# The first weight load of a decode layer, split into 16 and 112 partitions

## The chip, the cores and the metric

The kernel runs on one core of a Trainium2 chip. The metric is the device time of one execution in microseconds; shown is the median of several runs. A profile is one more execution with the hardware profiler on. Its span runs from the first to the last instruction of the program, and the time of that execution is slightly longer than the span.

## The reference

One decode step of a transformer layer with attention and a gated MLP side by side, all in float32, for one token `x` of 1024 elements:

```python
xn = _layernorm(x, axis=-1)
# A: attention over the last W = 4096 of 65536 cached positions, 32 query heads, 4 key/value heads
q = (xn @ wq)                                  # wq: 1024 x 4096
k, v = k_cache[:, :, Sk - W:, :], v_cache[:, :, Sk - W:, :]
p = softmax(q k^T * Dh ** -0.5)
a = (p v) @ wo                                 # wo: 4096 x 1024
# B: GEGLU
h = gelu(xn @ w_gate) * (xn @ w_up)            # both 1024 x 3584
b = h @ w_down                                 # 3584 x 1024
return x + a + b
```

With one token every weight is used once, so some 94 MB are read from HBM for each execution.

## The kernel before

All weights and the window of the two caches pass through one SBUF tensor, `ring`, of 128 partitions and 176 KB in each. The list `pieces` names the loads in order, with kind, index, place in the ring and size per partition in KB: `q` 0 and `q` 1 (the two halves of `wq`, 8 MiB each), `k` 0, `g` 0 (`w_gate`), `v` 0, `k` 1, `g` 1, `u` 0 (`w_up`), `v` 1, `u` 1, `o` 0 and 1 (`wo`), and the pieces `d` of `w_down`. `load` issues the DMA of a piece on SP's queue (through `dma`, L219), and `pump` issues as many pieces as find their place in the ring free; `done` frees a piece's place and pumps again. So SP's queue has a fixed order, and an instruction in it waits until the engines have done with what stood in that place. At the start `q` 0, `q` 1 and `k` 0 fit at once; `g` 0 takes the place of `q` 0.

The half `q` 0 is 512 rows of `wq`. `rows` puts four of them in each partition, so a partition receives one run of 4 x 4096 floats, 64 KB:

```python
    def rows(w, a):
        return w[512 * a:512 * (a + 1), :].rearrange("(p r) n -> p (r n)", r=4)
```

`project("q", 0)` multiplies it with the normed token on VectorE (DVE): for each of the four rows in a partition one instruction over 128 x 4096 adds the row times a scalar per partition to the accumulator `part` (the first a TENSOR_SCALAR at L209, the others a SCALAR_TENSOR_TENSOR at L213). `project("q", 1)` does the same with the second half, `projected("q")` adds up over the partitions on TensorE, and the queries go on to the scores.

`Program` records every operation with the regions that it reads and writes, and works out from the regions which earlier operations it has to wait for. Each DMA has a semaphore of its own (`s_dma` and its number among the operations), and a reader of a region waits for every DMA that wrote a part of it.

Of the kernel before, what the change touches and what calls it, by code (L numbers as in the profile page):

```python
# [10 lines left out]
P = 128  # L11
# [135 lines left out]
def decode_layer(nc, x, k_cache, v_cache, wq, wo, w_gate, w_up, w_down, out):  # L147
# [69 lines left out]
    def dma(engine, o, i, reads=(), writes=(), tag=None):  # L217
        return prog.add(
            engine, lambda e: e.dma_start(o, i), list(reads), list(writes), dma=True, tag=tag  # L219
        )  # L220
# [4 lines left out]
    def rows(w, a):  # L225
        return w[512 * a:512 * (a + 1), :].rearrange("(p r) n -> p (r n)", r=4)

    def heads_of(a):
        return wo[2048 * a:2048 * (a + 1), :].rearrange("(p t) n -> p (t n)", p=P)
# [14 lines left out]
    def load(kind, i, at, size):  # L244
        slot = ring[:, at * KB:(at + size) * KB]
        held[kind, i] = slot
        if kind == "v":
            src = v_cache[0, 2 * i:2 * i + 2, SK - WIN:, :].rearrange("g (p j) d -> p g (j d)", p=P)
            dma("sp", slot.rearrange("p (g n) -> p g n", g=2), src, writes=[slot], tag=(kind, i))
        elif kind == "k":  # L250
            src = k_cache[0, 2 * i:2 * i + 2, SK - WIN:, :].rearrange("g (s j) d -> s g (j d)", g=2, j=64)
            dma("sp", slot, src, writes=[slot], tag=(kind, i))
        elif kind == "d":
            lo, hi = i
            halves = 2 if lo == TD - 1 else 1
            wide = slot.rearrange("p (t n) -> p t n", n=D)
            for half in range(halves):
                cols = slice(half * D // halves, (half + 1) * D // halves)
                dst = wide[:, :, cols]
                dma("sp", dst, hidden_rows[:, lo:hi, cols], writes=[dst], tag=(kind, i, half))  # L260
        else:
            src = {
                "q": lambda: rows(wq, i), "g": lambda: rows(w_gate, i), "u": lambda: rows(w_up, i),
                "o": lambda: heads_of(i),
            }[kind]()
            dma("sp", slot, src, writes=[slot], tag=(kind, i))

    queue = list(pieces)
    live = {}
# [1 line left out]
    def pump():  # L271
        while queue:
            kind, i, at, size = queue[0]
            if any(at < hi and lo < at + size for lo, hi in live.values()):
                return
            load(*queue.pop(0))
            live[kind, i] = (at, at + size)
# [436 lines left out]
    for half in range(2):  # L714
        half_on_pe(column(27), held["d", (27, 28)], half, False, True)
        add(y[:, half, :], acc[:, half, :P], x_out[:, half, :])
        for k, engine in enumerate(("sp", "act")):
            src = y[31 + 64 * k:33 + 64 * k, half, :]
            dma(
                engine, stores[0, half, 2 * k:2 * k + 2, :], src, reads=[src],  # L720
                tag=("out", half, k),
# [26 lines left out]
```

## Time and profile before

| | |
|---|---|
| median of 3 runs | 226.75 us (226.56 to 226.86) |
| the profiled execution | 226.83 us, its span 225.5 us |
| bytes read from HBM | 94.38 MB, 419 GB/s over the span |
| busy DVE, PE, ACT | 143.2, 87.5, 26.3 us |
| SP's DMA queue (q1) | 97.5% of 16 DMA engines over the span |
| the two `A_wq` issues on SP | 0.41 us each |

The page's slices are fortieths of the span, with busy shares in tenths. In the chain of waits each piece stands with its start, its length, and what it was: a transfer, an engine's work at a line, or "issue", in which nothing shown was waited for. In the timeline the bracket behind a row gives how long the engine was idle before it and what ended that.

### The profile page before, as it was taken

To read this page: it belongs to the slowest core of one execution; us is meant where nothing else is said; L and a number is where in the kernel's file an instruction comes from. 1 tells how busy PE (TensorE), PEld (TensorE's weight loads), DVE (VectorE), ACT (ScalarE), POOL (GpSimd) and SP (SyncE) were. 2 spreads that over 40 slices of the span, in tenths; PEclk is the share of its full clock that TensorE was granted. 3 is DMA by queue.
4 is the path that set the end of the run, shared out by engine and by line. 5 is a ranking of instruction groups with operands and counts; after the bars stand their busy time and mean duration, and the time that the engine had idled before them with its cause. 6 is when DMAs were issued, how large, how long until landed. Compare 5 with 4: busy or idle time off the path is not lost.

```text
span 225.5 us, 1396 instructions
## 1 busy us (share of the span) xinstructions
PE 87.5 (39%) x574; PEld 34.8 (15%) x574; DVE 143.2 (64%) x127; ACT 26.3 (12%) x45; POOL 0.7 (0%) x6
## 2 busy tenths in 40 slices
PE   1200000007699007989002537137339204408475
PEld 0100000006263002462000111011002001002131
DVE  7500998499727990000998699869538804938691
ACT  2000000004555001482000300200000000000000
POOL 1000000000000000000000000000000000000000
PEclk9999999999999755999755667857855855965889
DMA  9899899899989999999999998999999999999992
GB/s 373 372 395 535 372 395 535 349 405 478 468 349 426 465 401 503 427 397 471 427 397 392 433 509 387 478 391 491 419 395 488 419 395 413 427 439 442 382 405 111
DMA packets 3317, 94.46 MB, mean 419 GB/s; under 512 B 350, under 2 KB 366, under 8 KB 1008
## 3 DMA queue, kind: packets, MB, share of 16 engines
q1 hardware_dynamic: 3288, 94.38, 97.5%
q8 instruction: 4, 0.07, 0.1%
q10 hardware_dynamic: 24, 0.01, 0.0%
q14 instruction: 1, 0.01, 0.0%
HBM read 94.38 MB, written 0.00 MB: 419 GB/s over the span
## 4 chain that ended last, share of the span: by engine, by line
DMA 65%; DVE 26%; PE 7%; issue 1%; SPq 1%; DVEq 0%
DVE part L213 24%; DMA ring<-in_B_w_down 19%; DMA ring<-in_A_wq 18%; DMA ring<-in_B_w_gate 15%; DMA ring<-in_A_wo 13%; PE acc L158 3%; PE tp L163 2%; PE s_p L158 2%; DVE part L209 1%; SPq L219 1%; DVE rows_sb L186 0%; DVE part L189 0%; DVEq L118 0%; SPq L118 0%
## 5 line engine op out<-in xcount | busy, mean ns | idle before, releaser
L213 DVE SCALAR_TENSOR_TENSOR part<-ring,xz,part 128x3584 f32<-128x3584 f32 (+1 forms) x19 | 78.8, 4148 | 26.6 <-DMA ring<-in_B_w_gate 22.6
L163 PE MATMUL tp<-ident,ring 128*128 128x128 f32 x128 | 20.3, 303 | 44.4 <-DMA ring<-in_A_k_cache 42.8
L213 DVE SCALAR_TENSOR_TENSOR part<-ring,oz,part 128x1024 f32<-128x1024 f32 x15 | 19.3, 1285 | 9.9 <-DMA ring<-in_A_wo 9.4
L172 ACT ACTIVATE ring<-tp 128x512 f32<-128x512 f32 x32 | 18.1, 596 | 58.4 <-PE tp L163 58.0
L163 PEld LDWEIGHTS tp<-ident,ring 128*128 128x128 f32 x128 | 15.0, 152 | 51.2 <-DMA ring<-in_A_k_cache 42.9
L209 DVE TENSOR_SCALAR part<-ring,xz 128x3584 f32<-128x3584 f32 (+1 forms) x3 | 6.5, 2176 | 19.7 <-DMA ring<-in_A_wq 12.1
L158 PE MATMUL acc<-ring,oz 128*32 128x512 f32 x64 | 11.7, 899 | 16.8 <-DMA ring<-in_A_wo 16.8
L213 DVE SCALAR_TENSOR_TENSOR part<-ring,hz,part 128x1024 f32<-128x1024 f32 x10 | 12.8, 1285 | 6.1 <-DMA ring<-in_B_w_down 5.8
L158 PE MATMUL acc<-part,unit 128*32 128x448 f32 (+1 forms) x48 | 7.3, 742 | 22.3 <-DVE part L213 22.3
L158 PE MATMUL o_p<-ring,pT 128*32 128x512 f32 x64 | 11.0, 847 | 7.1 <-DMA ring<-in_A_v_cache 6.5
L158 PE MATMUL acc<-ring,hz 128*32 128x128 f32 (+1 forms) x60 | 8.0, 616 | 10.1 <-DMA ring<-in_B_w_down 10.1
L158 PE MATMUL s_p<-ring,qz 128*32 128x512 f32 x64 | 9.3, 598 | 0.0
L163 PE MATMUL tp<-ident,rows_sb 128*128 128x128 f32 x16 | 3.5, 361 | 12.0 <-ACT rows_sb L172 11.8
L158 PE MATMUL sums<-ring,hz 128*32 128x256 f32 x72 | 6.2, 482 | 4.7 <-DMA ring<-in_B_w_down 4.7
L158 PEld LDWEIGHTS acc<-ring,oz 128*32 128x32 f32 x64 | 2.5, 155 | 26.6 <-DMA ring<-in_A_wo 19.4
L158 PEld LDWEIGHTS acc<-part,unit 128*32 128x32 f32 x48 | 1.4, 126 | 26.4 <-DVE part L213 24.2
L172 ACT ACTIVATE rows_sb<-s_p,negm 128x512 f32<-128x512 f32 x2 | 1.4, 687 | 30.4 <-DVE negm L209 30.4
L158 PEld LDWEIGHTS o_p<-ring,pT 128*32 128x32 f32 x64 | 2.6, 149 | 14.5 <-issue 13.4
L158 PE MATMUL acc<-ring,xz 128*32 128x448 f32 x32 | 4.8, 767 | 0.0
L158 PEld LDWEIGHTS acc<-ring,hz 128*32 128x32 f32 x60 | 2.2, 135 | 15.8 <-issue 14.0
L163 PEld LDWEIGHTS tp<-ident,rows_sb 128*128 128x128 f32 x16 | 2.3, 179 | 15.5 <-ACT rows_sb L172 13.6
L158 PEld LDWEIGHTS sums<-ring,hz 128*32 128x32 f32 x72 | 2.4, 136 | 9.2 <-DMA ring<-in_B_w_down 7.3
(85 smaller groups left out, 47.8 us busy)
## 6 DMA issues: line engine op xcount, KB each, us to landing
ring<-in_B_w_gate SPq DMA_DIRECT2D x2, 7168.0 KB, 31.9
ring<-in_B_w_up SPq DMA_DIRECT2D x2, 7168.0 KB, 33.9
ring<-in_A_k_cache SPq DMA_DIRECT2D x2, 4096.0 KB, 39.7
ring<-in_A_v_cache SPq DMA_DIRECT2D x2, 4096.0 KB, 34.8
ring<-in_B_w_down SPq DMA_DIRECT2D x1, 6144.0 KB, 42.9
ring<-in_B_w_down SPq DMA_DIRECT2D x1, 4096.0 KB, 38.8
ring<-in_B_w_down SPq DMA_DIRECT2D x2, 1024.0 KB, 40.4
ring<-in_B_w_down SPq DMA_DIRECT2D x3, 512.0 KB, 42.0
```

The costliest lines, as they stand in the source:

```text
L158: "pe", lambda e: e.matmul(o, lhsT, rhs, start=start, stop=stop),
L163: prog.add("pe", lambda e: e.transpose(o, i, eye), [i, eye], [o])
L172: "act", lambda e: e.activation(o, i, func, scale=scale, **kw),
L209: dve(lambda e: e.tensor_scalar(o, i, s1, s2, op0=op0, **kw), reads, [o])
L213: lambda e: e.scalar_tensor_tensor(o, i, factor, other, op0=ALU.mult, op1=ALU.add),
L219: engine, lambda e: e.dma_start(o, i), list(reads), list(writes), dma=True, tag=tag
```

## The change

The load of `q` 0, the first of the kernel, is issued as two transfers: partitions 0 to 15 (1 MiB), then partitions 16 to 127 (7 MiB). All other loads go as before.

```diff
-            dma("sp", slot, src, writes=[slot], tag=(kind, i))
+            cuts = [0, 16, P] if (kind, i) == ("q", 0) else [0, P]
+            for lo, hi in zip(cuts, cuts[1:]):
+                dma("sp", slot[lo:hi, :], src[lo:hi, :], writes=[slot[lo:hi, :]], tag=(kind, i))
```

On SP, at the head of the program, the order with the shape of each transfer (partitions x elements) is, before:

```order
L219 DMA ring<-in_A_wq 128x16384 [waits barrier_Pool_Activation_PE_DVE_SP_release]
L219 DMA ring<-in_A_wq 128x16384
L219 DMA ring<-in_A_k_cache 128x1x8192
L219 DMA ring<-in_B_w_gate 128x14336 [waits s_dve]
L219 DMA ring<-in_A_v_cache 128x2x4096 [waits s_dve]
```

and now:

```order
L219 DMA ring<-in_A_wq 16x16384 [waits barrier_Pool_Activation_PE_DVE_SP_release]
L219 DMA ring<-in_A_wq 112x16384
L219 DMA ring<-in_A_wq 128x16384
L219 DMA ring<-in_A_k_cache 128x1x8192
L219 DMA ring<-in_B_w_gate 128x14336 [waits s_dve]
```

One transfer more stands ahead of `q` 1. On DVE, where the projection of `q` begins, the difference is:

```order
 L195 TENSOR_TENSOR st<-st 128x1 [waits s_dve]
 L209 TENSOR_SCALAR xz<-xc,st 128x8 [waits s_dve]
-L209 TENSOR_SCALAR part<-ring,xz 128x4096 [waits s_dma4,s_dve]
+L209 TENSOR_SCALAR part<-ring,xz 128x4096 [waits s_dma4,s_dma5,s_dve]
 L213 SCALAR_TENSOR_TENSOR part<-ring,xz,part 128x4096 [waits s_dve] x3
-L213 SCALAR_TENSOR_TENSOR part<-ring,xz,part 128x4096 [waits s_dma5,s_dve]
+L213 SCALAR_TENSOR_TENSOR part<-ring,xz,part 128x4096 [waits s_dma6,s_dve]
```

The first instruction that reads `q` 0 waits for both of its transfers (`s_dma4` and `s_dma5`); all later DMA semaphores have a number one higher, and nothing else moves.

## The prediction

> **What bounds the kernel now.** I read the page first, for what is busy from end to end.
>
> ```profile
> span 225.5 us, 1396 instructions
> DMA  9899899899989999999999998999999999999992
> q1 hardware_dynamic: 3288, 94.38, 97.5%
> DMA 65%; DVE 26%; PE 7%; issue 1%; SPq 1%; DVEq 0%
> ```
>
> The transfers fill every slice to 0.8 or more until the last one, nearly all of them on queue q1, the one that SP issues to: 97.5% of what 16 DMA engines could have been busy. The 26% of DVE on the chain says less than it seems to; whether DVE or the transfers set the pace at the start is seen in the chain of waits in order of time, at its beginning and its end.
>
> ```profile
> 0.67 0.06 issue
> 0.73 0.41 SPq L219
> 1.14 0.06 issue
> 1.20 41.05 DMA ring<-in_A_wq
> ...
> 180.50 42.73 DMA ring<-in_B_w_down
> 223.23 0.04 issue
> 223.28 0.47 PE acc L158 x8
> ```
>
> The chain goes back to the two transfers of `A_wq`, issued within 1.2 us. At the other end the last landing, at 223.23, is followed by little more than eight matmuls. All of the last loads had been issued by 180.50, 43 us ahead. The next view is the timeline around the first loads, and the DMA view of the start for how deep the queue is.
>
> ```profile
> 23.00 2.35 DVE L209 TENSOR_SCALAR part<-ring,xz 128x4096 f32<-128x4096 f32 x1 [12.13 <-DMA ring<-in_A_wq]
> 25.39 13.53 DVE L213 SCALAR_TENSOR_TENSOR part<-ring,xz,part 128x4096 f32<-128x4096 f32 x3
> 38.94 0.33 SPq L219 DMA_DIRECT2D ring<-in_B_w_gate  x1
> 42.34 4.49 DVE L213 SCALAR_TENSOR_TENSOR part<-ring,xz,part 128x4096 f32<-128x4096 f32 x1 [3.43 <-DMA ring<-in_A_wq]
> ...
> ring<-in_A_k_cache SPq DMA_DIRECT2D x1, 4096.0 KB, 50.3
> ```
>
> DVE waits 12.13 us for the first load and 3.43 us for the second. The two releases lie 42.34 - 23.00 = 19.34 us apart, for 8 MiB. Each is 128 rows of 64 KB. SP issues the next load, `g` 0, at 38.94, when DVE is done with `q` 0. The first `k` load was issued at about 1.7 and landed 50.3 later, at 52. So 13 us of transfers still stand in the queue when `g` 0 joins it. The stream never runs dry, and a delay of the first load moves all that follows by as much: DVE, the issue of `g` 0 and the landing of `k` move together, and the 13 us stay.
>
> What one row takes, and how the rows are dealt out, is in the table by stretches (after the length of a stretch come five engines' busy time, granted clock, DMA share and GB/s; bytes are counted where a row starts).
>
> ```profile
> 1.50:2.00 0.50, 0.00 (x0) 0.00 (x0) 0.42 (x2) 0.07 (x1) 0.00 (x0) 1.00 4.34 1450
> 2.00:2.50 0.50, 0.26 (x3) 0.29 (x3) 0.36 (x2) 0.50 (x1) 0.00 (x0) 1.00 1.56 524
> 2.50:3.00 0.50, 0.35 (x3) 0.26 (x3) 0.50 (x1) 0.50 (x1) 0.00 (x0) 1.00 0.30 131
> 3.00:4.60 1.60, 0.00 (x0) 0.00 (x0) 1.39 (x5) 0.21 (x1) 0.00 (x0) 1.00 0.00 0
> 4.60:5.70 1.10, 0.00 (x0) 0.00 (x0) 0.96 (x7) 0.00 (x0) 0.00 (x0) 1.00 2.20 953
> 221.00:222.00 1.00, 0.42 (x8) 0.00 (x0) 0.42 (x1) 0.00 (x0) 0.00 (x0) 1.00 0.40 154
> 222.00:223.00 1.00, 0.97 (x24) 0.53 (x24) 0.00 (x0) 0.00 (x0) 0.00 (x0) 1.00 0.12 45
> ```
>
> 1450 GB/s over 0.5 us are 0.725 MB, or 11 rows of 65,536 bytes. Then 4 and 1 start, none from 3.00 to 4.60, and then 953 x 1.1 = 1.05 MB, the next 16. So 16 DMA engines take one row each, and eight in a row make the load: **19.34 / 8 = 2.42 us for a row**, 27.1 GB/s on each engine. The last rows of the table show how the kernel ends: one engine's share is 1/16 = 0.06, so in the last microsecond only about two engines still work. The engine that is latest sets the end.
>
> **The change, part by part.**
>
> *One more issue on SP.* An `A_wq` issue takes 0.41 us (the chain's second row). The second load and the first `k` come 0.4 us later into a queue that holds 8 MiB, 19 us of work. Cost nothing; even uncovered it would be 0.4. What the completion of one transfer more takes on the engines no row shows apart; the rows follow in bursts without room for much, so I take 0 and leave some tenths to the range.
>
> *One more wait on DVE.* The first TENSOR_SCALAR at L209 now waits for two semaphores. Queued behind it is all of DVE's work, and behind that SP's issue of `g` 0. If both have come, another wait is like the chain's 0.03 to 0.06 us of "issue", hidden by the 3.43 us for which DVE waits again before `q` 1. 0.
>
> *The first piece, 16 rows.* In bytes nothing changes: 1 + 7 rows for an engine instead of 8. What changes is where they are written at one time. All large transfers in this trace write 128 partitions, and no row shows 16 neighbours being written by 16 engines, so 27.1 GB/s may be the limit of an engine or of the stretch of partitions that it writes. If the engine limits, the piece takes one row's time, 2.42 us, and the cost is 0. If the receiving side limits, there are 16 stretches of eight partitions with 27.1 GB/s each. Sixteen neighbours lie in 2 stretches if a stretch is eight neighbours, which gives 8 rows' times (19.36 us); in 4 if a stretch takes its partitions by fours (9.68 us); in 16 if it takes them one by one (2.42 us again). So the ends are 0 and +16.9 us. No row lies near either. I take the middle, four rows' times: 3 x 2.42 = 7.26 us more. All engines share in that delay, since each carries one of the 16 rows.
>
> [...]
>
> *The second piece, 112 rows.* Each engine has seven, most simply seven neighbours: 16 to 22, 23 to 29 and so on. Against the receiving side's limit such shares no longer match stretches of eight. The stretches that got nothing from the first piece still have eight rows to take, so 8 rows' times are the least. If two engines met in a stretch all the time, the seven rows would take 14. That engines meet throughout is unlikely, as shares of seven step through the stretches and 16 stretches stand against 16 engines; I take 9.5 for the engine that ends last, in the lower part of 8 to 14. [...]
>
> *Sum.* 4 + 9.5 = 13.5 rows' times instead of 8: 5.5 x 2.42 = **13.3 us**, and all that follows moves by it. The profiled execution took 226.83 (span 225.5 and 1.3 around it); the median of the three runs is 226.75, 0.08 less. Span 238.8, time 240.1, rounded to **240**. By the same working with 8 and 11 the time is 236.4 (+9.7) and 243.7 (+16.9). Work behind the stream takes none of this back: the stream is the bound, it has no idle stretch, and DVE's spare 3.43 us lie behind the landing.
>
> **Rivals.**
>
> *Only the first piece is late.* The 112 rows run at seven rows' times, because engines that are ahead go on to `q` 1 and let the others pass: 7.26 us, 234.0.
>
> *Stretches of eight neighbours.* Two stretches for 16 rows, then 8 to 10 for the rest: 16 to 18 rows' times, +19.4 to +24.2, 246 to 251. For it: the simplest layout of 128 partitions on 16 engines. Against it: nothing in the trace.
>
> *The 112 rows are dealt out one by one*, so that 16 neighbours are written at every step: 7 x 4 + 4 = 32 rows' times, +58 us, 285.
>
> *The engine is the limit, and the split does nothing.* For it: the rows come in even bursts of 16, as from engines with a fixed rate; but stretches with a fixed rate would show the same. 226.8, and within 0.45 us of 226.75, which is 0.2%, about what a measurement of this kernel can tell from no change.
>
> *A sooner start, faster.* The engine is the limit, and a first transfer of one row an engine is handed out sooner. Now 11 engines start by 2.00, four by 2.50 and the last after that, and each engine's lateness stays with it, since the rows follow without a gap. If all started in the first of these stretches, the last would gain 0.5 to 1.0 us; engines that are late at the end may be others, so I count 0.6: 226.1. It decides if the last engine ends over 0.45 us earlier and the first piece's rows take 2.42 us. By the receiving side's limit it is lost in 7 us.
>
> **How the numbers follow.** The forecast (four stretches, 8 to 11 rows' times for the rest, 236.4 to 243.7) has 0.60, since the rows leave 0 to +16.9 open for the first piece and the middle layout is what I chose. The first piece alone late: 0.10. Eight neighbours: 0.11. Dealt one by one: 0.05. No effect: 0.08. Sooner start: 0.04. Slower for a reason that I don't name: 0.02. So faster 0.04, same 0.08, slower 0.88. [...] The likeliest is 240. The range goes from 231, 3 us under the first piece alone, to 250, which takes in most of eight neighbours. It leaves out 0.17 of the cases named and a little of their edges.
>
> **What would show it.** In the changed profile the first 16 rows start together near 1.8, and the next 16 not by 5.7 but from about 11 us on. DVE's wait before its first TENSOR_SCALAR grows from 12.13 to 25 us, and the operation starts near 36. The 3.43 us before `q` 1 and the spacing of `g` 0 from it stay within a microsecond or two. Rows after `q` 0 take 2.42 us again, and the last landing is at about 236.5. The prediction is wrong if the second 16 rows start before 6 us (the engine is the limit), or if the first row takes other than about four times 2.42 us (another layout). It is also wrong if DVE starts on time and something else is late, or if the delay at the start is larger than that at the end, which would mean slack in the stream that I don't see.

## The result, and the profile after

The changed kernel takes 247.06 us (246.83 to 247.26) against 226.76 for the kernel before: a ratio of 1.0897, 95% interval 1.0883 to 1.0911, or 20.3 us more. The forecast of 240 had the direction and the place right and two thirds of the size.

The page of the changed kernel, with the GB/s in fortieths of the span:

```profile
span 245.9 us, 1397 instructions
DMA  9879898899999979999999899999999999999993
GB/s 171 171 171 320 192 256 235 373 480 405 437 473 438 448 318 450 434 473 438 448 432 438 372 397 520 438 392 430 472 394 469 394 469 424 400 424 416 404 409 139
q1 hardware_dynamic: 3304, 94.38, 97.7%
```

The DMA engines look as busy as before (97.7% on q1, before 97.5%). "Busy" only says that a row is under way, not how fast it goes: in the first seven slices, 43 us, the engines show 0.7 to 0.9 busy and move 171 to 320 GB/s. From the ninth slice on, the last one apart, the rates are 318 to 520 GB/s, much as before. A busy share alone would have hidden the whole loss.

The timeline around the first loads and the end of the chain of waits:

```profile
44.72 2.35 DVE L209 TENSOR_SCALAR part<-ring,xz 128x4096 f32<-128x4096 f32 x1 [33.86 <-DMA ring<-in_A_wq]
47.11 13.53 DVE L213 SCALAR_TENSOR_TENSOR part<-ring,xz,part 128x4096 f32<-128x4096 f32 x3
60.66 0.35 SPq L219 DMA_DIRECT2D ring<-in_B_w_gate  x1
64.09 9.00 DVE L213 SCALAR_TENSOR_TENSOR part<-ring,xz,part 128x4096 f32<-128x4096 f32 x2 [3.45 <-DMA ring<-in_A_wq]
...
201.01 42.67 DMA ring<-in_B_w_down
243.69 0.04 issue
243.73 0.47 PE acc L158 x8
```

DVE's first operation on `q` 0 starts at 44.72 instead of 23.00, 21.72 us later. What comes next keeps its distance: `g` 0 is issued 15.94 us after that start, as before, and the wait for `q` 1 is 3.45 us instead of 3.43. The last landing is at 243.69 instead of 223.23, 20.46 later.

The table by stretches shows the rows themselves (DMA share and GB/s are its last two columns). Sixteen rows start in each filled stretch, one on each engine, so share times length is the mean time of a row:

```profile
1.50:3.00 1.50, 0.61 (x4) 0.55 (x4) 1.27 (x3) 1.05 (x1) 0.00 (x0) 1.00 5.71 702
3.00:9.50 6.50, 1.18 (x4) 1.01 (x4) 4.54 (x23) 0.31 (x2) 0.00 (x0) 1.00 0.00 0
9.50:11.50 2.00, 0.00 (x0) 0.00 (x0) 1.03 (x6) 0.12 (x1) 0.00 (x0) 1.00 2.66 524
11.50:15.30 3.80, 0.00 (x0) 0.00 (x0) 0.00 (x0) 0.00 (x0) 0.00 (x0) 1.00 0.00 0
15.30:16.50 1.20, 0.00 (x0) 0.00 (x0) 0.00 (x0) 0.00 (x0) 0.00 (x0) 1.00 4.01 875
20.10:21.20 1.10, 0.00 (x0) 0.00 (x0) 0.00 (x0) 0.00 (x0) 0.00 (x0) 1.00 2.91 954
23.40:25.80 2.40, 0.00 (x0) 0.00 (x0) 0.00 (x0) 0.00 (x0) 0.00 (x0) 1.00 1.60 437
27.20:29.40 2.20, 0.00 (x0) 0.00 (x0) 0.00 (x0) 0.00 (x0) 0.00 (x0) 1.00 2.07 477
31.45:34.10 2.65, 0.00 (x0) 0.00 (x0) 0.00 (x0) 0.00 (x0) 0.00 (x0) 1.00 1.79 396
36.20:38.80 2.60, 0.00 (x0) 0.00 (x0) 0.00 (x0) 0.00 (x0) 0.00 (x0) 1.00 1.76 403
```

The first rows, those of the 16 partitions, take 5.71 x 1.50 = 8.6 us in the mean, and the next ones start between 9.5 and 11.5. Then come the seven rows of each engine for the 112 partitions, with 5.3, 4.8, 3.2, 3.8, 4.6, 4.7 and 4.6 us, 31.0 in sum. None of these means comes down to 2.42 us, the row of the kernel before.

### The profile page after: what moved, and what is told of

Read it like the earlier page. It is cut to its first block, busy times and chain, and to the rows that moved or that the text cites. A ratio compares the mean times of both kernels' runs of the same rounds, so it can differ in the third digit from the quotient of the medians.

```text
span 245.9 us, 1397 instructions
## 1 busy us (share of the span) xinstructions
PE 85.9 (35%) x574; PEld 34.7 (14%) x574; DVE 143.2 (58%) x127; ACT 26.2 (11%) x45; POOL 0.7 (0%) x6
## 3 DMA queue, kind: packets, MB, share of 16 engines
q1 hardware_dynamic: 3304, 94.38, 97.7%
## 4 chain that ended last, share of the span: by engine, by line
DMA 60%; DVE 30%; PE 6%; another core or an unknown queue 1%; issue 1%; SPq 0%; DVEq 0%
DVE part L213 28%; DMA ring<-in_A_wq 18%; DMA ring<-in_B_w_down 17%; DMA ring<-in_B_w_gate 13%; DMA ring<-in_A_wo 12%; PE acc L158 2%; PE tp L163 2%; DVE part L209 2%; PE s_p L158 2%; SPq L219 0%; DVE rows_sb L186 0%; DVE part L189 0%; DVEq L118 0%; SPq L118 0%
## 5 line engine op out<-in xcount | busy, mean ns | idle before, releaser
L213 DVE SCALAR_TENSOR_TENSOR part<-ring,xz,part 128x3584 f32<-128x3584 f32 (+1 forms) x19 | 78.8, 4148 | 25.6 <-DMA ring<-in_B_w_gate 21.6
L158 PE MATMUL acc<-ring,oz 128*32 128x512 f32 x64 | 10.5, 814 | 17.4 <-DMA ring<-in_A_wo 17.4
L213 DVE SCALAR_TENSOR_TENSOR part<-ring,hz,part 128x1024 f32<-128x1024 f32 x10 | 12.8, 1285 | 6.2 <-DMA ring<-in_B_w_down 5.9
L158 PE MATMUL acc<-part,unit 128*32 128x448 f32 (+1 forms) x48 | 8.4, 835 | 21.4 <-DVE part L213 21.4
L158 PE MATMUL acc<-ring,hz 128*32 128x128 f32 (+1 forms) x60 | 6.5, 530 | 9.9 <-DMA ring<-in_B_w_down 9.9
L163 PE MATMUL tp<-ident,rows_sb 128*128 128x128 f32 x16 | 3.5, 360 | 11.7 <-ACT rows_sb L172 11.5
L158 PEld LDWEIGHTS acc<-ring,hz 128*32 128x32 f32 x60 | 2.0, 125 | 14.6 <-issue 12.8
```

Of the source, the lines that this page charges most:

```text
L158: "pe", lambda e: e.matmul(o, lhsT, rhs, start=start, stop=stop),
L163: prog.add("pe", lambda e: e.transpose(o, i, eye), [i, eye], [o])
L213: lambda e: e.scalar_tensor_tensor(o, i, factor, other, op0=ALU.mult, op1=ALU.add),
```

## The experiments

The theory: a DMA engine's 27.1 GB/s are those of the stretch of partitions that it writes to (taken to be four neighbours and the four that lie 32 further on, an assumption that the runs below test); engines that write to one stretch share them. (A stretch is from here on such a group of eight partitions; in "the table by stretches" it is one of time.) Its rivals: a second transfer costs this much as such; rows that lie close together in HBM are read slowly; the number of partitions in a transfer sets its rate.

**A cut by columns.** Two transfers of 1 and 7 MiB again, but both over all partitions. Against the changed kernel:

```diff
-            cuts = [0, 16, P] if (kind, i) == ("q", 0) else [0, P]
+            cuts = [0, 8 * KB, size * KB] if (kind, i) == ("q", 0) else [0, size * KB]
             for lo, hi in zip(cuts, cuts[1:]):
-                dma("sp", slot[lo:hi, :], src[lo:hi, :], writes=[slot[lo:hi, :]], tag=(kind, i))
+                dma("sp", slot[:, lo:hi], src[:, lo:hi], writes=[slot[:, lo:hi]], tag=(kind, i))
```

> The first load is again two transfers of 1 MiB and 7 MiB, but cut by columns: each writes all 128 partitions (8 KB and 56 KB of each). Receiving side as the limit: all 16 stretches are written at all times, so 226.8 us, within 0.5 of the kernel before. Cost of a second transfer as such (issue, completion, second wait): slower by the 20 us that the split by partitions cost, or a good part of it. Source side: rows are read in the same spacing as before, no change.

226.52 us, ratio 0.9988 (0.9978 to 0.9997). The same bytes, issues and waits as in the changed kernel cost nothing, so a second transfer as such is not the cause. It is even faster by 0.1%, and the first load lands 0.45 us sooner, as the timeline shows (23.00 before):

```profile
22.55 2.35 DVE L209 TENSOR_SCALAR part<-ring,xz 128x4096 f32<-128x4096 f32 x1 [11.69 <-DMA ring<-in_A_wq]
```

**Two halves**, `cuts = [0, 64, P]`:

> The first load is cut into partitions 0 to 63 and 64 to 127. Receiving side, stretches of four neighbours and four 32 further on: each half reaches 8 of 16 stretches, so its four rows an engine take eight rows' times; 16 x 2.42 = 38.7 us instead of 19.4, 246 us in all. Source side (engines that read rows close to each other in HBM): the halves are read in wider spacing than the 16 rows were, so little loss, under 232. Second transfer as such: 247, as with 16 and 112.

248.18 us, ratio 1.0945 (1.0923 to 1.0967). In the table by stretches two bursts of rows stand alone:

```profile
3.00:9.50 6.50, 1.17 (x4) 1.00 (x4) 4.54 (x23) 0.29 (x2) 0.00 (x0) 1.00 0.79 161
11.50:15.30 3.80, 0.00 (x0) 0.00 (x0) 0.00 (x0) 0.00 (x0) 0.00 (x0) 1.00 1.35 276
```

161 GB/s x 6.5 us and 276 x 3.8 are 16 rows each, with 5.1 us a row: 0.79 x 6.50 and 1.35 x 3.80. All engines run at a little under half speed (5.1 us a row against 2.42), as with eight stretches for 16 engines. The time is 2 us over the 246 expected, as 5.13 is 6% over twice 2.42. A fixed cost of a second transfer, which would have given 247, had already fallen with the cut by columns.

**Other source rows for the same partitions** (against the kernel before):

```diff
-            dma("sp", slot, src, writes=[slot], tag=(kind, i))
+            if (kind, i) == ("q", 0):
+                blocks = src.rearrange("(i j) n -> i j n", j=8)
+                dma("sp", slot[0:16, :], blocks[:, 0, :], writes=[slot[0:16, :]], tag=(kind, i))
+                dma("sp", slot[16:P, :], blocks[:, 1:8, :], writes=[slot[16:P, :]], tag=(kind, i))
+            else:
+                dma("sp", slot, src, writes=[slot], tag=(kind, i))
```

> 16 and 112 partitions as in the changed kernel, but the 16 rows that go to partitions 0 to 15 are taken from every eighth row of the source, and the rest goes to partitions 16 to 127 in order (so the query projection is computed with weight rows in exchanged places). Receiving side: the rows' times stay, 8 to 9 us for the first, and the time is 247 within 1. Source side: the first rows no longer take 8 to 9 us, and the total moves by several us.

246.91 us, ratio 1.0888 (1.0867 to 1.0910), as with neighbouring rows. The first 16 rows take 8.5 us in the mean (8.6 in the changed kernel). The timeline's row for DVE's first operation says the same (44.72 in the changed kernel):

```profile
44.47 2.35 DVE L209 TENSOR_SCALAR part<-ring,xz 128x4096 f32<-128x4096 f32 x1 [33.61 <-DMA ring<-in_A_wq]
```

With the source rows so far apart nothing changes, so that rows lie close together in HBM is not the cause.

**Transfers by themselves.** Eight loads from `wq` ahead of the first one, each waiting for the one before:

```diff
+    probe_slot = ring[:, :64 * KB]
+    near = rows(wq, 0)
+    far = near.rearrange("(i j) n -> i j n", j=8)[:, 0, :]
+    for dst, src in (
+        (ring[0:P, :64 * KB], near), (ring[0:16, :64 * KB], near[0:16, :]), (ring[0:16, :64 * KB], far),
+        (ring[0:P:8, :64 * KB], near[0:16, :]), (ring[0:112:7, :64 * KB], near[0:16, :]),
+        (ring[0:112:7, :64 * KB], far), (ring[0:64, :64 * KB], near[0:64, :]),
+        (ring[16:P, :64 * KB], near[16:P, :]),
+    ):
+        dma("sp", dst, src, writes=[probe_slot])
     pump()
```

> Eight transfers of 64 KB rows ahead of the first load, one at a time, each waiting for the one before; the rest as before. Issue to landing, with about 2.5 us around the rows' own time: (1) 128 partitions 22 in all theories. Receiving side with groups of four: (2) partitions 0-15 from neighbouring source rows 12; (3) partitions 0-15 from every eighth source row 12; (4) every eighth partition 7, since 8 stretches are reached; (5) every seventh partition, 14 stretches, 5 to 7; (6) the same from every eighth source row 5 to 7; (7) partitions 0-63 22; (8) partitions 16-127 25 to 36. Source side: (2), (4) and (5) alike at 11, (3) and (6) alike at another value. Engine as the limit: 5 for all five of 16 rows, 12 for (7), 19.5 for (8).

The chain of waits has one piece for each, from issue to landing:

```profile
0.73 22.32 DMA ring<-in_A_wq
...
23.07 11.52 DMA ring<-in_A_wq
...
34.61 11.59 DMA ring<-in_A_wq
...
46.21 7.53 DMA ring<-in_A_wq
...
53.76 7.14 DMA ring<-in_A_wq
...
60.92 7.11 DMA ring<-in_A_wq
...
68.04 22.84 DMA ring<-in_A_wq
...
90.90 33.46 DMA ring<-in_A_wq
```

Sixteen neighbours take 11.52 us, and 11.59 with source rows far apart. The same 1 MiB to every eighth partition takes 7.53. So the partitions written decide, and 64 partitions (22.84) take as long as 128 (22.32). But 112 partitions need 11 us more than all 128. And every seventh partition, where at most four of 16 rows share a stretch, took 7.14 and 7.11: at 0.73 x 5.80 = 4.2 us a row in the mean, and 3.76 to 4.74 us row by row in the first of the two, all 16 were slow. Sharing alone does not give that.

**Smaller transfers**, in place of those eight, with first partition, step and count:

```diff
+    for first, step, count in (
+        (32, 4, 16), (11, 7, 16), (30, 4, 16), (0, 4, 8), (64, 4, 8), (0, 1, 4), (0, 1, 2), (0, 64, 2),
+    ):
+        dst = ring[first:first + step * (count - 1) + 1:step, :64 * KB]
+        dma("sp", dst, near[0:count, :], writes=[probe_slot])
```

> Eight small transfers of 64 KB rows ahead of the first load, one at a time; the rest as before. In the first probes, 16 rows on 14 stretches took 7.1 us to land, though at most four of them shared a stretch. Three readings. Sharing alone: a row alone on its stretch takes 2.42 us whoever writes it. Home: an engine is slower on a stretch that is not the one it writes in a load of 128 partitions, even alone there. Coupling: rows that are alone are held up by others that share. Issue to landing, with 2.2 us around the row: (1) partitions 32, 36 ... 92, 16 stretches, each engine on its home stretch: 4.7 in all readings (a little more, as it is the first). (2) partitions 11, 18 ... 116, 16 stretches, engines not at home: sharing and coupling 4.7, home 6 or more. (3) partitions 30, 34 ... 90, 15 stretches, one shared by two, nobody at home: sharing 7.1 at the end with 14 rows at 2.42; coupling 7.1 with all rows late; home as in (2). (4) 8 rows at 0, 4 ... 28: 4.7. (5) 8 rows at 64, 68 ... 92, not at home: 4.7, home 6 or more. (6) partitions 0 to 3: 11.9. (7) 0 and 1: 7. (8) 0 and 64: 4.7, home 5 or more for the second.

From issue to landing in this order the chain of waits has 5.29, 5.16, 7.31, 5.03, 4.99, 11.04, 6.35 and 5.18 us. The second writes 16 stretches and, if the rows are dealt out in order as the expectation takes it, from other engines than a load of 128 partitions does. It is no slower than the first, and the fifth no slower than the fourth, so "home" falls. Four rows in one stretch (partitions 0 to 3) take 11.04, nearly as long as 16 rows in four stretches do: it is the stretch that counts, not the size of the transfer. Two rows in one stretch took 6.35, where 7 was expected. With one shared stretch (the third, 7.31) the mean row took 0.49 x 6.10 = 3.0 us; row by row the trace has two of 4.26 and 4.83 us and 14 of 2.4 to 3.1, so only two were late, as many as share. Coupling as I had put it, with all rows late, did not show there; two shared stretches had not been tried in steps.

**How many stretches are shared**, 0 to 4 by the first partition (only the list differs from the last one):

```diff
+        (32, 4, 16), (28, 4, 16), (24, 4, 16), (20, 4, 16), (16, 4, 16), (11, 7, 16), (3, 7, 16), (2, 7, 16),
```

> Eight transfers of 16 rows of 64 KB, one at a time, ahead of the first load; they differ in how many stretches are written by two engines at once: partitions from 32, 28, 24, 20 and 16 on in steps of four (0, 1, 2, 3 and 4 shared stretches), then from 11, 3 and 2 on in steps of seven (0, 1 and 2). Rows alone in the earlier probes took 2.4 to 3.4 us. Sharing alone: only the rows that share take 4.3 to 5, two for each shared stretch, all others 2.4 to 3.4. Coupling: with one shared stretch 14 rows stay at 2.4 to 3.4; from two on, all 16 rows take 3.8 or more, as with every seventh partition from 0 on (two shared stretches, 3.76 to 4.74).

The table by stretches, one row for each transfer in this order:

```profile
2.00:5.90 3.90, 0.61 (x4) 0.55 (x4) 3.41 (x14) 1.26 (x1) 0.00 (x0) 1.00 0.73 270
7.20:12.70 5.50, 1.07 (x4) 0.90 (x4) 1.91 (x11) 0.20 (x1) 0.00 (x0) 1.00 0.55 191
14.00:19.90 5.90, 0.00 (x0) 0.00 (x0) 0.00 (x0) 0.00 (x0) 0.00 (x0) 1.00 0.72 178
21.00:27.20 6.20, 0.00 (x0) 0.00 (x0) 0.00 (x0) 0.00 (x0) 0.00 (x0) 1.00 0.75 169
28.30:34.60 6.30, 0.00 (x0) 0.00 (x0) 0.00 (x0) 0.00 (x0) 0.00 (x0) 1.00 0.76 166
35.80:39.90 4.10, 0.00 (x0) 0.00 (x0) 0.00 (x0) 0.00 (x0) 0.00 (x0) 1.00 0.71 256
41.00:47.00 6.00, 0.00 (x0) 0.00 (x0) 0.00 (x0) 0.00 (x0) 0.00 (x0) 1.00 0.50 175
48.00:54.40 6.40, 0.00 (x0) 0.00 (x0) 0.00 (x0) 0.00 (x0) 0.00 (x0) 1.00 0.69 164
```

Share times length, the mean row: 2.85 us with no shared stretch, 3.03 with one, 4.25 with two, 4.65 with three, 4.79 with four; in steps of seven 2.91, 3.00 and 4.42 with none, one and two. If only the sharing rows were slow, at some 4.5 us, two shared stretches would give (12 x 2.85 + 4 x 4.5) / 16 = 3.3. Row by row the difference is plain: with one shared stretch (the second transfer) two rows take 3.82 and 4.25 us and the other 14 take 2.5 to 3.2; with two (the third) all 16 take 3.8 to 4.5. So from two crowded stretches on, the other twelve engines are held up as well. That fewer stretches are written is not enough for it: eight rows on eight stretches landed in 5.03 us. What holds the others up, no run here shows.

**Three pieces**, `cuts = [0, 32, 96, P]`:

> The first load is cut into partitions 0-31, 32-95 and 96-127. Stretches of four neighbours and four 32 further: the middle transfer is 64 partitions that reach all 16 stretches, four rows an engine at 2.42 us, where 64 partitions from 0 on took 5.12 us a row; the outer two reach 8 stretches, two rows an engine at 5.12 us each. 10.2 + 9.7 + 10.2 = 30.1 us instead of 19.4: 237.5, within 2. If it is the number of partitions in a transfer that counts, all rows take 5.12: 41 us, 248.

237.73 us, ratio 1.0487 (1.0468 to 1.0506), where 237.5 was expected. The table by stretches over the second row of an engine in the first piece, and the second and third in the middle one:

```profile
6.00:8.00 2.00, 0.59 (x2) 0.50 (x2) 1.25 (x8) 0.00 (x0) 0.00 (x0) 1.00 2.56 524
...
14.40:15.60 1.20, 0.00 (x0) 0.00 (x0) 0.00 (x0) 0.00 (x0) 0.00 (x0) 1.00 2.02 874
17.00:17.80 0.80, 0.00 (x0) 0.00 (x0) 0.00 (x0) 0.00 (x0) 0.00 (x0) 1.00 3.03 1312
```

2.56 x 2.00 = 5.1 us for partitions 0 to 31; 2.02 x 1.20 = 3.03 x 0.80 = 2.42 us for 32 to 95. By the theory's layout, partitions 32 to 95 reach all 16 stretches and ran at the kernel's 2.42 us a row; partitions 0 to 63 (the halves) reach eight and took 5.13.

**Cutting by columns at other places.** At 1 KB (`KB` in place of `8 * KB`):

> The cut by columns with a smaller first transfer, 1 KB of each of the 128 partitions instead of 8 KB, then 63 KB. With 8 KB the first load landed 0.45 us sooner and the kernel was faster by 0.1%. If that gain comes from short first rows, which let the 16 engines begin closer together, it stays or grows: 226.3 to 226.6. If the eight first rows of 1 KB take more than their bytes, it is lost: 226.8 or over.

226.99 us, ratio 1.0016 (1.0007 to 1.0025): the gain is lost. The first load landed later than before, with DVE's start at 23.20. At 8 KB again:

> The cut by columns of 8 and 56 KB once more, in more rounds: 226.5, faster by 0.1%, if the earlier gain was real; 226.7 if not.

226.62, ratio 0.9990 (0.9981 to 0.9999): the small gain was there again. At 16 KB:

> The cut by columns at 16 KB, the end of the first of the four rows in a partition, so that DVE's first operation waits for 2 MiB instead of 8. It starts near 11 us, when the normed token is ready, instead of 23.0, and DVE is done with q 0 about 2.4 us sooner. Since transfers are the bound and 13 us of them stand in the queue when g 0 joins it, none of the 2.4 us comes through: 226.5, as with the cut at 8 KB. If DVE set the pace at the start, 224.4.

226.59, ratio 0.9992 (0.9983 to 1.0001), not told from no change. DVE starts at 10.90 instead of 23.00 and has the first operation out of the way. It then waits 9.40 and 5.81 us, where the kernel before waits 12.13 and 3.43, as the timeline shows:

```profile
10.90 2.35 DVE L209 TENSOR_SCALAR part<-ring,xz 128x4096 f32<-128x4096 f32 x1
22.65 13.52 DVE L213 SCALAR_TENSOR_TENSOR part<-ring,xz,part 128x4096 f32<-128x4096 f32 x3 [9.40 <-DMA ring<-in_A_wq]
36.20 0.33 SPq L219 DMA_DIRECT2D ring<-in_B_w_gate  x1
41.99 4.49 DVE L213 SCALAR_TENSOR_TENSOR part<-ring,xz,part 128x4096 f32<-128x4096 f32 x1 [5.81 <-DMA ring<-in_A_wq]
```

`g` 0 is issued 2.74 us sooner than before (36.20 instead of 38.94) and the kernel ends with the others: transfers are the bound.

## Why the prediction was right, and where not

**The time: inside the range by luck.** The measured 247.06 lies in the range of 231 to 250, but above 243.7, where my own working ended with 11 rows' times for the second piece. The range reached so far only to take in the stretches of eight neighbours, a layout that the probes exclude.

**The bound and the cover: right.** All but 1.3 us of the delay went through to the end, behind an unchanged 3.45 us of DVE's second wait. The 16 KB cut shows it from the other side, with DVE done 2.74 us sooner for nothing.

**The issue on SP and the wait on DVE at 0: right.** The cut by columns has both and is not slower (226.52 us, ratio 0.9988).

**The first piece, four rows' times: right, and so was the middle layout.** 9.68 us was forecast. No row of the kernel before had decided for this layout: it was the middle of the three that I had named. The rows took 8.6 in the mean and were all done by 11.5, when the last of the next rows had begun. The source and the size of the transfer are excluded as causes. Groups of four, with four more 32 further on, say which probes were fast: 16 rows from partition 32 on in steps of four, with no stretch shared, took 2.85 us in the mean, and from 16 on, with four shared, 4.79; partitions 32 to 95 ran at 2.42 us a row, and the halves at 5.13, which is 16 x 65,536 bytes in that time, or 204 GB/s.

**The second piece, 9.5 rows' times: this term failed.** The 19.34 us of the load before and the 21.72 us of delay at DVE's start make 41.06 us, 17.0 rows' times. With four for the first piece, 13 are left for the second, 3.5 more than I took, or 8.5 us. I had put 8 to 14 as the ends and argued for the lower part, since two engines meet only part of the time. They do, by that layout: but I let the engines that meet nobody run at 2.42 us. In the last probes, from two crowded stretches on, all 16 slowed down, to 4.2 to 4.8 us a row in the mean. If an engine's share is seven neighbours (16 to 22, 23 to 29 and so on), the layout by fours, worked through row by row, has two such stretches in the first, second, fifth, sixth and seventh row of the second piece, and one in the third and fourth. The table by stretches of the changed kernel has 5.3, 4.8, 4.6, 4.7 and 4.6 us for the five, and 3.2 and 3.8 for the two. All seven rows fit; that the shares are cut so was not shown in another way. Sharing alone, walked through with the engines in step, gives an estimated 8.5 rows' times in the mean and 10 for the worst share. The 11 rows' times behind the forecast's upper end, 243.7, are shown by no run; in their place the rows took 31.0 us in the mean, 12.8 rows' times. That is how the conflict of a few engines became everybody's.

**Given back: 1.3 us, not foreseen.** From DVE's first operation on `q` 0 to the last landing it was 223.23 - 23.00 = 200.2 us, and 243.69 - 44.72 = 199.0 after. So the delay at the start is larger than that at the end, one of the prediction's signs of being wrong, which was to mean slack in the stream. The traces show another reason: the engines are not alike late. The table by stretches shows when they go on from `q` 0 to `q` 1:

```profile
40.90:42.45 1.55, 0.00 (x0) 0.00 (x0) 0.00 (x0) 0.00 (x0) 0.00 (x0) 1.00 1.81 592
42.45:43.65 1.20, 0.00 (x0) 0.00 (x0) 0.00 (x0) 0.00 (x0) 0.00 (x0) 1.00 0.30 109
```

592 x 1.55 and 109 x 1.20 are 14 rows and 2. Two engines go on only at 43.5, over a microsecond behind the others, and DVE waits for them; in the kernel before all 16 go on within a microsecond (21.6 to 22.6). The stream as a whole is less late than DVE from then on: counted by the bytes whose transfer has begun, by 20.3 us at 20 and at 40 MB and 20.6 at 60 MB, against 20.46 at the end. With the halves (244.65 - 44.40) and the three pieces (234.02 - 33.67), where all engines are delayed alike, the distance stays 200.3. In sum: 13.3 + 8.5 - 1.3 = 20.5, measured 20.3.

**The rivals.** Stretches of eight neighbours would have given 246 to 251, which holds the measured time, for a reason that the probes exclude: 16 neighbours took 8.6 us in the mean, near four rows' times (9.68) and not eight (19.36). The first piece alone, rows dealt one by one, and the engine as the limit fall with the table by stretches of the changed kernel. The sooner start is real in a cut that leaves all stretches in use: 0.45 us at the landing of the first load and 0.1% in time with 8 KB, nothing gained with 1 KB. That cut by columns is the one version that beats both kernels, by a margin under the 0.2% that I had set.

**The signs to look for.** The second 16 rows began between 9.5 and 11.5, as said. DVE's wait grew to 33.86 instead of 25 us and the last landing came at 243.69 instead of 236.5, both by the second piece. Of the signs of being wrong, only the larger delay at the start came out, for the reason given above.

## What to carry to other kernels

Cut a transfer along the free dimension and not along the partitions: with the same bytes, issues and waits one cost nothing here (226.52 us against 226.83) and the other 20.3 us. If partitions must be cut, look for pieces that reach all stretches evenly, as 32 to 95 did by this layout (2.42 us a row); the pieces on either side of it did not (5.1 us a row for 0 to 31, 4.9 for the first rows of 96 to 127), and no run here cut a whole load by partitions without loss. When DMA engines show as busy, look at the GB/s beside it: 0.7 to 0.9 busy went with 171 to 320 GB/s in the first seven slices here. And where several stretches are crowded at once, price the conflict for all engines and not only for those that meet: with two crowded stretches all 16 rows took 3.8 to 4.5 us, with none 2.85 in the mean.

## What the runs showed that I had not expected

Two crowded stretches slowed the engines that write elsewhere (mean row 4.25 and 4.42 us), while one did not (3.03 and 3.00, against 2.85 and 2.91 with none). In the halves, where by the layout two engines share a stretch all the time, a row took 5.13 us, 6% over twice 2.42. And with a first transfer of short rows the whole first load lands 0.45 us sooner if its rows are 8 KB, but 0.20 us later if they are 1 KB (DVE's start at 22.55 and 23.20, against 23.00).
